# Later weight fetches tied to units, one pair of heads whole in batches 0 and 1, another estimate for transposes

## The chip, the cores and the metric

The kernel runs on one core of a Trainium2 chip. The core has engines that run side by side, each through its own instructions in their order: TensorE (PE in the profile; PEld is its weight load) multiplies matrices, VectorE (DVE), ScalarE (ACT) and GpSimd (POOL) work on elements, and SyncE (SP) here issues the DMAs. The metric is the time of one execution on the device in microseconds (us).

## The reference

Attention in which a query sees only the keys of its own hash bucket, and behind it two dense layers with a squared ReLU:

```python
q_bits = (np.einsum('bhsd,dk->bhsk', q, proj) > 0).astype(np.int64)   # k likewise
q_bucket = np.sum(q_bits * powers, axis=-1)
mask = q_bucket[:, :, :, None] == k_bucket[:, :, None, :]
scores = scale * np.matmul(q, k.transpose(0, 1, 3, 2))
scores = np.where(mask, scores, -1000000000.0)
attn = np.exp(scores - np.max(scores, axis=-1, keepdims=True))
attn = attn / (np.sum(attn, axis=-1, keepdims=True) + 1e-09)
...
x = np.ascontiguousarray(attn_out.transpose(0, 2, 1, 3)).reshape(B * S, H * D)
h = np.maximum(x @ w_in, 0.0)
return (h * h @ w_out).astype(np.float32)
```

There are 4 batches, 8 heads, 768 tokens and 64 elements in a head; `x` is 3072 x 512, `w_in` 512 x 2048 and `w_out` 2048 x 512, drawn in float64 and brought to the chip as they are.

## The kernel before

The Python program records operations and doesn't issue them. `Program.add` (line 148) notes each operation with the buffers that it reads and writes, the engines that could do it ("ways"), and a rank. `order` (222) then plans: `forward` (295) places operations in time on five queues by the estimated costs of `cost` (174) and one estimate for all DMA, `backward` (251) gives priorities from the end of that plan, and of five rounds the one with the shortest planned span is kept. `emit` (376) issues each engine's operations in the planned order. What the planner believes of a duration thus changes no instruction, only their order on each engine, and for operations with several ways the engine. The emitted program keeps the true dependences of data; each engine takes its instructions in the order given.

**Units and visits.** The attention of one head is done in two halves of 384 queries, each in three units of 128. A `unit` (651) makes scores `pS` on PE, their negated maximum `nmx` on DVE, `e` = exp with its sum on ACT, the reciprocal `rv`, two fp16 parts `hl` (ACT, then DVE), and a transposing DMA from `hl` to `aT`. There are 192 units. A visit is a pair of heads and one half, so six units. Behind them `av` (679) multiplies `aT` with the values `VV` into `pA` and leaves two parts in `xx`. `prep` (564) makes a pair's operands `A`, `L`, `Q` and `M`, of which two buffers each exist. In batch 0 it is "plain": one prep takes one buffer of each (its first head `A` and `L`, its second `Q` and `M`), so the last two preps are alive. A later prep takes both buffers of all four, and only the last is alive. When the next visit's pair is no longer alive, `ready` (792) prepares it again.

The order of visits (785 to 788): `WHOLE` says of how many pairs of a batch both halves come one after the other. The other pairs come first with half 0, and then, backwards, with half 1. Batches that aren't named have all four pairs whole. Before, batch 0 has two whole pairs: its order is pair 0 both halves, 1 both halves, 2 and 3 with half 0, 3 and 2 with half 1.

**The MoE.** When all four pairs of a batch's half are done, `moe` (696) runs a stage, eight in all. A stage has 16 blocks of `w_in`: `pm` on PE, then `g32` and the two parts `g` on ACT and DVE, and the second layer into `po`. A step is a group of three matmuls; a block has four steps into `pm` and three into `po`, so a stage has 112 steps, and the kernel 896. `pace` (770) ties step m to a unit u by the points of `PACE`: the planner places the step only after that unit's first matmul. Beyond the last point steps are free. Only the first stage finds weights that aren't aligned yet: it sums four blocks at a time into `acc`, and `align` (546) then scales `wo` in place.

**Weights.** Each layer has four groups of four tiles. `fetch` (489) loads a 512 KB tile of raw 64-bit numbers (`raw`, two buffers), takes sixteen bits of each (`top`, on DVE or POOL), and makes `f` on DVE; `split` (515) squares the four `f` on ACT (`sq`), adds them on PE (`pt`) for a scale, and writes two fp16 parts into `win` or `wo`. Group 0 and 1 of `w_in` and group 0 of `w_out` are recorded behind the first three visits (`WIN_AT`, `WOUT_AT`), the others inside the first stage (757 to 763), all with ranks of their own.

**Around it.** While the planned order leaves PE idle ahead of the first `pm`, `emit` fills in `idle` matmuls. In odd units below `ALTERNATE`, `pS` uses the PSUM space of `po`.

Of the kernel before, what the change touches and what calls it, by code (L numbers as in the profile page):

```python
# [40 lines left out]
ROUNDS, BEHIND = 4, 40000  # L41

PREP, STACKS, VALUES = -9, 0, 2
WIN_RANK, WOUT_RANK = (18, 2.0), (30, 2.5)
RANK_PE, RANK_MOE = 1e6, -1.0

PLAIN, ALTERNATE = 4, 36

WHOLE = {0: 2}


WIN_AT, WOUT_AT = (0, 2), 1
FIRST = len(WIN_AT)

PACE = ((25, 0), (64, 120), (193, 640))

IDLE_FROM, IDLE_SHARE = 1000, 0.6

# [54 lines left out]
class Program:  # L113
# [59 lines left out]
    @staticmethod  # L173
    def cost(key, name, args, kw):

        size = lambda x: int(np.prod(x.shape[1:]))
        column = {F32: 4 / 2.4, F32R: 0.445}
        if name == "matmuls":

            side = {32: 4, 64: 2}.get(size(args[0][0][1]), 1)  # L180
            t = sum(size(a[2]) * column.get(a[2].dtype, 1 / 2.4) + 7 for a, _ in args) / side
            return t, t
        kinds = [x.rec.kind if isinstance(x, View) else "" for x in args]
        ptr = any(isinstance(x, View) and x.shape[-1] == 1 for x in args[2:3])
        n = max(size(args[0]), size(args[1]) if isinstance(args[1], View) else 0)
        if key == "pe":
            t = max(107, size(args[2]) * column.get(args[2].dtype, 1 / 2.4) + 3)
            return t, t
        if name.startswith("dma"):
            b = int(np.prod(args[0].shape)) * mybir.dt.size(args[0].dtype)  # L190
            inside = name == "dma_start_transpose" or kinds[:2] == ["sb", "sb"]
            busy = 1040 if key == "pool" else (650 if inside else 475) + 50 * (key == "act")
            return busy, b / (175 if name == "dma_start_transpose" else 314)
        if key == "act":
            t = 93 * (isinstance(kw.get("scale"), View) + isinstance(kw.get("bias"), View)) + (51 if "psum" in kinds[:2] else 93) + n / 1.2 + 93 * ("accum_out" in kw)
        elif key == "pool":
            t = 147 + n * (2.1 if args[0].dtype == F32 or args[0].dtype == F32R else 1.88) if name == "tensor_tensor" else 161 + n / 1.2 + 83 * ptr
        else:
            fast = name in ("tensor_copy", "tensor_scalar") and "psum" not in kinds[:2]
            both = len(args) > 3 and isinstance(args[3], View) and args[3].shape[-1] == 1  # L200
            t = 67 + n / (1.92 if fast else 0.96) + 62 * (ptr and (fast or name == "scalar_tensor_tensor")) + 100 * both
        return t, t
# [212 lines left out]
def lsh_attention_moe(ctx: ExitStack, tc, kq, v, proj2, w_in, w_out, consts, out):  # L415
# [10 lines left out]
    def send(out, x):  # L426
        sp.dma_start(out, x)
# [58 lines left out]
        dve.memset(x.bitcast(F32), 0.0)  # L486
    turn = [0]

    def fetch(src):

        raw = sb([P, 512, 2], U32, "raw", BUFS["raw"])
        send(raw.rearrange("p n t -> p (n t)").bitcast(U16)[:, 0:2047], src.bitcast(U16)[:, 1:2048])
        first = tops[turn[0] % len(tops)]
        turn[0] += 1
        move(first[:, :, 1], raw.rearrange("p n t -> p (n t)").bitcast(BF16).rearrange("p (n t) -> p n t", t=4)[:, :, 2], 1.0, (dve, pool))
        f = sb([P, 512], F32, "f")
        dve.scalar_tensor_tensor(f.bitcast(U32), raw[:, :, 0], 13, first.rearrange("p n t -> p (n t)").bitcast(U32), ALU.logical_shift_right, ALU.bitwise_or)
        return f
# [13 lines left out]
        dve.tensor_scalar(back, norm, 2.0**50, 1.0, ALU.mult, ALU.mult)  # L512
        return to, back

    def split(srcs, parts, name):

        fs = [fetch(src) for src in srcs]
        pt = ps([P, 512], F32, "pt", tag="misc")
        for n, f in enumerate(fs):
            sq = sb([P, 512], BF16, "sq", 2)  # L520
            square(sq, f)
            pe.matmul(pt, ones, sq, start=n == 0, stop=n == len(fs) - 1)
        norm = sb([P, 1], F32, "norm")
        dve.tensor_reduce(norm, pt, AX.X, ALU.max)
        to, back = scales(norm, name, 4)
        for f, (hi, lo) in zip(fs, parts):
            move(hi, f, to)
            left(lo, f, to, hi)
        return to, back
# [2 lines left out]

    def split_win(j):
        w = slice(j * 512, (j + 1) * 512)
        win_back.append(split([w_in[:, cc, w] for cc in range(NCC)], [(win[:, 0, cc, w], win[:, 1, cc, w]) for cc in range(NCC)], "win")[1])

    def split_wout(j):

        back = split([w_out[:, n] for n in range(4 * j, 4 * j + 4)], [(wo[:, 0, n], wo[:, 1, n]) for n in range(4 * j, 4 * j + 4)], "wo")[1]
        z = zs[:, j : j + 1]  # L540
        dve.tensor_scalar(z, back, win_back[j], win_back[j], ALU.mult, ALU.mult)

# [153 lines left out]
    def moe(n, b, half):  # L696
# [5 lines left out]
        for f in range(NF + 1):  # L702
            if f < NF:
                pr.rank = RANK_PE
                pm = ps([P, 512], F32, "pm", 1)
                pr.busy_from = min(pr.busy_from, len(pr.ops))
                for cc in reversed(range(NCC)):
                    pr.mark = pace()
                    wh = win[:, 0, cc, f * P : (f + 1) * P]
                    wl = win[:, 1, cc, f * P : (f + 1) * P]  # L710
                    pe.matmul(pm[:, 0:HS], wh, X[cc][:, 0], start=cc == NCC - 1, stop=False)
                    pe.matmul(pm[:, 0:HS], wh, X[cc][:, 1], start=False, stop=False)
                    pe.matmul(pm[:, 0:HS], wl, X[cc][:, 0], start=False, stop=cc == 0)
                pr.rank, pr.mark = RANK_MOE, None

                g32 = sb([P, HS], F32, "g32", 2)
                pr.add((act, "activation", (g32, pm[:, 0:HS], AF.Relu), {"scale": 2.0**-23}),
                       (dve, "tensor_scalar", (g32, pm[:, 0:HS], 2.0**-23, 0.0, ALU.mult, ALU.max), {}))
                square(g32, g32)
                g = gs[f] = sb([P, 2, HS], F16, "g")  # L720
                move(g[:, 0], g32)
                left(g[:, 1], g32, 1.0, g[:, 0])

            if f > 0:
                m = f - 1
                g = gs.pop(m)
                pr.mark = None
                first, last = (m % 4 == 0, m % 4 == 3) if n == 0 else (m == 0, m == NF - 1)
                if first:
                    po = ps([P, 3, DM], F32, "po")  # L730
                for t in range(3):
                    gh = g[:, 0, t * P : (t + 1) * P]
                    gl = g[:, 1, t * P : (t + 1) * P]
                    pr.rank, pr.mark = RANK_PE, pace()
                    pe.matmul(po[:, t], gh, wo[:, 0, m], start=first, stop=False)
                    pe.matmul(po[:, t], gh, wo[:, 1, m], start=False, stop=False)
                    pe.matmul(po[:, t], gl, wo[:, 0, m], start=False, stop=last)
                    pr.mark = None
                pr.rank = RANK_MOE
                if n == 0 and last:  # L740
                    back = unscaled(b, m // 4)
                if n == 0 and m == 3:
                    acc = sb([P, 3, DM], F32, "acc")
                for t in range(3):
                    r0 = b * S + half * HS + t * P
                    if n == 0 and last:
                        if m == 3:
                            move(acc[:, t], po[:, t], back)
                        else:
                            dve.scalar_tensor_tensor(acc[:, t], po[:, t], back, acc[:, t], ALU.mult, ALU.add)  # L750
                        if m == NF - 1:
                            send(out[r0 : r0 + P], acc[:, t])
                    elif last:
                        o = sb([P, DM], F32, "o", tag="f")
                        move(o, po[:, t], back)
                        send(out[r0 : r0 + P], o)
            if n == 0 and f in (1, 5, 9):
                j = f // 4 + FIRST
                if j < 4:
                    pr.rank = win_rank(4 * j)  # L760
                    split_win(j)
                pr.rank = conv_rank(f + 3)
                split_wout(f // 4 + 1)
        if n == 0:
            pr.rank = RANK_MOE
# [4 lines left out]
    def pace():  # L770
# [3 lines left out]
            if m < m1:  # L774
                return int(u0 + (u1 - u0) * (m - m0) / (m1 - m0))
        return None

    def conv_rank(f):
        return WOUT_RANK[0] + WOUT_RANK[1] * f

    def win_rank(c):
        return WIN_RANK[0] + WIN_RANK[1] * c


    visits = []
# [11 lines left out]

    ready(*visits[0][:2], -10.0, PLAIN > 0)

    early = {n: (split_win, j, win_rank(4 * j)) for j, n in enumerate(WIN_AT)}  # L800
    early[WOUT_AT] = split_wout, 0, conv_rank(0)
    done, u, stages = {}, 0, 0
    for n, (b, hp, half) in enumerate(visits):
        sts, aTs = kept[b, hp], []
# [56 lines left out]
```

## Time and profile before

| what | us |
|---|---|
| median of 3 runs | 925.9 |
| lowest and highest of them | 923.61 and 926.62 |
| the profiled execution | 925.36 |
| its span, from the first to the last instruction | 923.6 |
| first `pm` of the MoE | 169.5 |
| DVE busy | 643.8 |
| ACT busy | 663.6 |

A row of a timeline has start, duration, engine, line, operation, what it writes and reads, and a count. A row of groups has a count, the busy time, the mean in ns, and the idle time in front of it with what ended that. A row of windows has the stretch, its length, each engine's busy time with instructions in brackets, PE's granted clock, the DMA engines' busy share and GB/s; asked for one tile, it counts that tile's instructions alone. As one helper records everything, most instructions have line 402, pairs of matmuls line 399 and idle matmuls line 395, so tiles tell more than lines.

### The profile page before, as it was taken

Reading aid. Unit: us, or ns where it says so; the run is one execution under the profiler, and the core shown is the slowest. Engines: PE = TensorE matmul, PEld = TensorE weight load, DVE = VectorE, ACT = ScalarE, POOL = GpSimd, SP = SyncE. Lnnn points to the kernel's source line nnn. Section 1 sums busy time; section 2 is a strip of 40 time slices with the busy share of each in tenths; the row PEclk is TensorE's granted clock in tenths of the full one; section 3 lists DMA queues with packets and bytes.
Section 4 is the critical chain, followed back from the end, with each engine's and each line's share of the span. In section 5 each row is a group of like instructions: output and inputs, shape, how many; then the busy total and the mean of one; then the engine's idle time right before and its main releaser. Section 6 shows DMA issues by size and latency. Waiting matters only on the chain.

```text
span 923.6 us, 15264 instructions
## 1 busy us (share of the span) xinstructions
PE 885.6 (96%) x5592; PEld 501.3 (54%) x5592; DVE 643.8 (70%) x1206; ACT 663.6 (72%) x1166; POOL 54.8 (6%) x104
## 2 busy tenths in 40 slices
PE   7988988999997999999999999999999999999997
PEld 6555555445554555555555556555555555554553
DVE  5999999988979687889686768797867651211111
ACT  4877987878879677888777768787778673533433
POOL 0111301200103000000000000000000000000000
PEclk9999999999999999999999999999999999999999
DMA  7998999997999797999697959897878640200000
GB/s 236 248 222 210 226 237 213 250 211 193 236 203 242 133 192 148 185 234 244 145 198 159 190 121 198 174 213 154 170 149 177 121 102 10 77 1 0 35 1 35
DMA packets 329323, 149.99 MB, mean 162 GB/s; under 512 B 305568, under 2 KB 305696, under 8 KB 329248
## 3 DMA queue, kind: packets, MB, share of 16 engines
q1 hardware_dynamic: 329248, 149.02, 73.6%
q8 instruction: 44, 0.72, 0.3%
q14 instruction: 31, 0.25, 0.1%
HBM read 43.59 MB, written 6.29 MB: 54 GB/s over the span
## 4 chain that ended last, share of the span: by engine, by line
PE 63%; ACT 5%; DMA 2%; DVE 2%; issue 1%; POOL 0%; SPq 0%; ACTq 0%; DVEq 0%
PE po L402 23%; PE pm L402 21%; PE pS L402 9%; PE pA L399 8%; ACT wo L402 1%; DMA aT<-hl 1%; ACT e L402 1%; PE pd L399 1%; DMA RV<-vp 1%; ACT hl L402 1%; DVE hl L402 1%; ACT g L402 1%; PE pc L402 1%; DVE nmx L402 1%; DMA M<-Q 1%
## 5 line engine op out<-in xcount | busy, mean ns | idle before, releaser
L402 PE MATMUL po<-wo,g 128*128 128x512 f16 x1152 | 332.7, 381 | 2.7 <-ACT wo L402 0.9
L402 PE MATMUL pm<-xx,win 128*128 128x384 f16 x1536 | 322.4, 327 | 1.3 <-DVE g L402 1.0
L402 DVE TENSOR_REDUCE nmx<-pS 128x1 f32<-128x768 f32 x192 | 183.1, 954 | 57.7 <-PE pS L402 56.6
L402 ACT ACTIVATE e<-pS,nmx 128x768 f32<-128x768 f32 x192 | 171.6, 894 | 67.8 <-DVE nmx L402 48.8
L402 DVE SCALAR_TENSOR_TENSOR hl<-e,rv,hl 128x768 f16<-128x768 f32 x192 | 194.1, 1012 | 26.1 <-ACT hl L402 25.5
L402 PEld LDWEIGHTS <-win 128*128 128x128 f16 x1536 | 145.1, 98 | 115.4 <-issue 17.8
L402 ACT ACTIVATE hl<-e,rv 128x768 f16<-128x768 f32 x188 | 173.5, 928 | 25.1 <-ACT e L402 14.0
L402 PEld LDWEIGHTS <-g 128*128 128x128 f16 x1152 | 107.9, 98 | 131.3 <-issue 26.4
L402 DVE SCALAR_TENSOR_TENSOR g<-g,g 128x384 f16<-128x384 f32 x122 | 67.5, 554 | 127.7 <-ACT g L402 127.1
L402 ACT ACTIVATE g<-pm 128x384 f32<-128x384 f32 x125 | 60.7, 486 | 108.3 <-PE pm L402 107.4
L402 ACT ACTIVATE g<-g 128x384 f32<-128x384 f32 (+1 forms) x248 | 128.8, 520 | 10.8 <-PE po L402 5.6
L399 PE MATMUL pA<-aT,VV 128*64 128x384 f16 x1152 | 117.8, 331 | 0.0
L402 PE MATMUL pS<-A,Q 128*128 128x384 f32 x288 | 95.2, 411 | 5.0 <-ACT e L402 4.8
L399 PEld LDWEIGHTS <-VV 128*64 128x64 f16 x1152 | 59.5, 109 | 55.8 <-issue 35.8
L402 PE MATMUL pS<-L,M 128*128 128x384 f32 x288 | 77.8, 350 | 0.2
L402 PEld LDWEIGHTS pS<-A,Q 128*128 128x128 f32 x288 | 49.3, 190 | 29.8 <-ACT e L402 15.9
L402 POOL TENSOR_SCALAR rv<-sm 128x1 f32<-128x1 f32 x74 | 28.8, 389 | 610.6 <-ACT e L402 604.0
L395 PEld LDWEIGHTS <-ones 128*128 128x128 bf16 x756 | 49.9, 103 | 20.1 <-issue 11.8
L395 PE MATMUL idle<-ones 128*128 128x128 bf16 x756 | 54.7, 228 | 2.7 <-DVE ones L402 2.7
L402 PEld LDWEIGHTS pS<-L,M 128*128 128x128 f32 x288 | 51.9, 189 | 3.9 <-issue 2.4
L402 PE MATMUL pS<-Q,M 128*128 128x384 f32 x96 | 37.3, 510 | 9.5 <-ACT e L402 9.1
L402 PE MATMUL pS<-A,L 128*128 128x384 f32 x96 | 36.6, 508 | 5.7 <-ACT e L402 5.4
(92 smaller groups left out, 579.9 us busy)
## 6 DMA issues: line engine op xcount, KB each, us to landing
RV<-vp SPq DMA_DIRECT2D x32, 384.0 KB
R<-kq SPq DMA_DIRECT2D x24, 384.0 KB
raw<-w_in SPq DMA_DIRECT2D x16, 511.8 KB
raw<-w_out SPq DMA_DIRECT2D x16, 511.8 KB
out<-o SPq DMA_DIRECT2D x21, 256.0 KB
Q<-L SPq DMA_DIRECT2D x24, 192.0 KB
Q<-A SPq DMA_DIRECT2D x24, 192.0 KB
L<-M SPq DMA_DIRECT2D x24, 192.0 KB
```

The lines of the kernel that those rows point to most:

```text
L395: issue(q, q.engine.matmul(self.idle[0].real(), self.idle[1].real(), self.idle[1].real(), start=True, stop=True).ins)
L399: ins = q.engine.matmul(*map(real, args), **kw).ins
L402: ins = getattr(q.engine, o.name)(*map(real, o.args), **{k: real(x) for k, x in o.kw.items()}).ins
```

## The change

- `WHOLE` is `{0: 1, 1: 1}`: in batches 0 and 1 one pair is whole, and the other three have half 0 first and half 1 backwards.
- Every fetch of a weight tile gets a mark: the planner places the load behind the first matmul of the unit in `WIN_FROM` or `WOUT_FROM` for its group. The ranks of the groups are listed one by one. As with `pace`, the mark is a dependence of the plan alone.
- ACT may take `top`.
- `PACE` runs in one line from unit 20 to 700 steps at unit 193.
- `ALTERNATE` ends at unit 30.
- The planner's bandwidth for a transposing DMA is 292 bytes per ns where it was 175.

```diff
-WIN_RANK, WOUT_RANK = (18, 2.0), (30, 2.5)
+WIN_RANK, WOUT_RANK = (18, 20, 28, 34), (20, 25, 31, 37)
+
+WIN_FROM, WOUT_FROM = (0, 18, 25, 31), (8, 22, 28, 34)
...
-PLAIN, ALTERNATE = 4, 36
-
-WHOLE = {0: 2}
+PLAIN, ALTERNATE = 4, 30
+
+WHOLE = {0: 1, 1: 1}
...
-PACE = ((25, 0), (64, 120), (193, 640))
+PACE = ((20, 0), (193, 700))
...
-            return busy, b / (175 if name == "dma_start_transpose" else 314)
+            return busy, b / (292 if name == "dma_start_transpose" else 314)
...
-    def fetch(src):
+    def fetch(src, since):
 
         raw = sb([P, 512, 2], U32, "raw", BUFS["raw"])
+        pr.mark = since
         send(raw.rearrange("p n t -> p (n t)").bitcast(U16)[:, 0:2047], src.bitcast(U16)[:, 1:2048])
+        pr.mark = None
...
-        move(first[:, :, 1], raw.rearrange("p n t -> p (n t)").bitcast(BF16).rearrange("p (n t) -> p n t", t=4)[:, :, 2], 1.0, (dve, pool))
+        move(first[:, :, 1], raw.rearrange("p n t -> p (n t)").bitcast(BF16).rearrange("p (n t) -> p n t", t=4)[:, :, 2], 1.0, (act, dve, pool))
...
-    def split(srcs, parts, name):
-
-        fs = [fetch(src) for src in srcs]
+    def split(srcs, parts, name, since):
+
+        fs = [fetch(src, since) for src in srcs]
...
                 if j < 4:
-                    pr.rank = win_rank(4 * j)
+                    pr.rank = WIN_RANK[j]
                     split_win(j)
-                pr.rank = conv_rank(f + 3)
+                pr.rank = WOUT_RANK[f // 4 + 1]
                 split_wout(f // 4 + 1)
...
-    early = {n: (split_win, j, win_rank(4 * j)) for j, n in enumerate(WIN_AT)}
-    early[WOUT_AT] = split_wout, 0, conv_rank(0)
+    early = {n: (split_win, j, WIN_RANK[j]) for j, n in enumerate(WIN_AT)}
+    early[WOUT_AT] = split_wout, 0, WOUT_RANK[0]
```

`split_win` and `split_wout` hand `WIN_FROM[j]` and `WOUT_FROM[j]` on to `split`; `conv_rank` and `win_rank` are gone.

More of the change, by code (lines that the diff above doesn't have):

```diff
@@ L534, in split_win @@
         w = slice(j * 512, (j + 1) * 512)
-        win_back.append(split([w_in[:, cc, w] for cc in range(NCC)], [(win[:, 0, cc, w], win[:, 1, cc, w]) for cc in range(NCC)], "win")[1])
+        win_back.append(split([w_in[:, cc, w] for cc in range(NCC)], [(win[:, 0, cc, w], win[:, 1, cc, w]) for cc in range(NCC)], "win", WIN_FROM[j])[1])
     def split_wout(j):
-        back = split([w_out[:, n] for n in range(4 * j, 4 * j + 4)], [(wo[:, 0, n], wo[:, 1, n]) for n in range(4 * j, 4 * j + 4)], "wo")[1]
+        back = split([w_out[:, n] for n in range(4 * j, 4 * j + 4)], [(wo[:, 0, n], wo[:, 1, n]) for n in range(4 * j, 4 * j + 4)], "wo", WOUT_FROM[j])[1]
         z = zs[:, j : j + 1]
@@ L776, in pace @@
         return None
[L778 to L782, printed above, removed]
     visits = []
```

## The prediction

> **What bounds the kernel now.** I read the page first: the span and the engines' row.
>
> ```profile
> span 923.6 us, 15264 instructions
> PE 885.6 (96%) x5592; PEld 501.3 (54%) x5592; DVE 643.8 (70%) x1206; ACT 663.6 (72%) x1166; POOL 54.8 (6%) x104
> ```
>
> TensorE (PE) is the engine to read, but 96% hides two stages. The windows show them (columns: busy PE, PEld, DVE, ACT, POOL; clock; DMA).
>
> ```profile
> 25.00:50.00 25.00, 22.75 (x177) 14.20 (x177) 24.80 (x51) 20.27 (x36) 4.40 (x9) 1.00 1.05 222
> 138.00:169.50 31.50, 26.57 (x251) 17.59 (x246) 30.10 (x61) 22.78 (x40) 5.07 (x8) 1.00 1.06 220
> 169.50:300.00 130.50, 122.93 (x730) 67.12 (x728) 118.21 (x228) 113.00 (x190) 18.27 (x31) 0.99 0.97 222
> 300.00:740.00 440.00, 438.50 (x2674) 247.59 (x2672) 336.10 (x607) 342.15 (x613) 11.64 (x26) 1.00 0.84 174
> L395 PE MATMUL idle<-ones 128*128 128x128 bf16 x756 | 54.7, 228 | 2.7 <-DVE ones L402 2.7
> DVE nmx L402 <- PE pS L402: 2.2, 6, 0.5
> ```
>
> Up to 169.5 us VectorE (DVE) is the bound: 24.80 of 25 us busy, and still 30.10 of 31.5 at the end; the longest of its waits between 25 and 169.5 us, the last row, comes to 2.2 us. TensorE's busy time there includes 756 idle matmuls, placed only ahead of the first `pm`. At 169.5 us the MoE begins, and from there TensorE is the bound.
>
> That it is full after 300 us I check by its work, not by its busy share. The prices first, from starts of neighbouring rows on PE, then the counts of matmuls.
>
> ```profile
> 59.13 1.56 PE L402 MATMUL pS<-Q,M 128*128 128x384 f32 x4
> 60.52 0.38 PE L402 MATMUL pt<-sq,ones 128*128 128x512 bf16 x1
> 60.74 2.45 PE L395 MATMUL idle<-ones 128*128 128x128 bf16 x41
> ...
> 70.97 3.12 PE L399 MATMUL pA<-aT,VV 128*64 128x384 f16 x36
> 74.02 0.39 PE L402 MATMUL pt<-sq,ones 128*128 128x512 bf16 x1
> ...
> 191.72 0.85 PE L399 MATMUL pd<-R,pj 128*32 128x384 f32 x8
> 192.50 1.15 PE L402 MATMUL pm<-xx,win 128*128 128x384 f16 x6
> ...
> 292.00 0.62 PE L402 MATMUL pS<-A,Q 128*128 128x384 f32 x2
> ...
> 292.81 1.96 PE L402 MATMUL pm<-xx,win 128*128 128x384 f16 x11
> ```
>
> A plain unit (batch 0) costs 60.52-59.13 = 1.39 us, an `av` 74.02-70.97 = 3.05, a `pt` of 512 columns 60.74-60.52 = 0.22, the `pd` of a prep 0.78 and its four `pc`, bf16 as `pt` but 384 wide, 0.22 x 384/512 = 0.16 each, so a prep 1.4, and a later unit 292.81-292.00 = 0.81.
>
> ```profile
> 300.00:740.00 440.00, 161.41 (x804) 1.00 0.84 174
> 760.00:910.00 150.00, 100.92 (x428) 1.00 0.07 19
> 300.00:740.00 440.00, 171.49 (x624) 1.00 0.84 174
> 760.00:910.00 150.00, 102.82 (x317) 1.00 0.07 19
> 300.00:740.00 440.00, 120.23 (x456) 1.00 0.84 174
> 300.00:740.00 440.00, 70.33 (x680) 1.00 0.84 174
> 760.00:910.00 150.00, 9.67 (x72) 1.00 0.07 19
> 300.00:740.00 440.00, 7.67 (x72) 1.00 0.84 174
> ```
>
> These are, in pairs, `pm` and `po`, then `pS`, `pA` (two) and `pd`. A step is three matmuls. From 760 to 910 us: (428+317)/3 = 248 steps in 150 us less two `av` and a last bit of `pS` (7), so 0.58 us a step. From 300 to 740 us: 476 steps x 0.58 = 276, 114 units x 0.81 = 92, 18.9 `av` x 3.05 = 58, 9 preps x 1.4 = 13. The sum is 439 of 440 us: PE is full. So only two things shorten this kernel: useful PE work done ahead of 169.5 us, and the 130.5-122.93 = 7.6 us in which PE stands still between 169.5 and 300.
>
> **The change, part by part.** *WHOLE.* In batch 0 the first half's fourth pair now comes with the fifth visit, not the sixth: 30 units instead of 36 ahead of MoE stage 0. When is that?
>
> ```profile
> 0.00:126.60 126.60, 30.34 (x30) 0.99 0.97 228
> 134.11 1.00 PE L399 MATMUL pA<-aT,VV 128*64 128x384 f16 x10
> 161.71 1.98 PE L399 MATMUL pA<-aT,VV 128*64 128x384 f16 x22
> 169.50 1.30 PE L402 MATMUL pm<-xx,win 128*128 128x384 f16 x7
> ```
>
> The first counts DVE's `hl`: the 30th ends at 126.6 us. From the 30th to its `av` took 134.1-126.6 = 7.5 us, and from the sixth `av` to the first `pm` 169.5-161.7 = 7.8. So 126.6+15.3 = 142 us, if DVE has done the same by then.
>
> *Top of the weights on ACT, marks, ranks.* DVE's own share before that point changes a little.
>
> ```profile
> L402 DVE TENSOR_SCALAR top<-raw 128x512 f16<-128x512 bf16 x16 | 7.3, 454 | 0.4 <-DMA raw<-w_in 0.3
> L402 DVE SCALAR_TENSOR_TENSOR f<-raw,top 128x512 uint32<-128x512 uint32 x28 | 19.4, 697 | 0.0
> L402 DVE SCALAR_TENSOR_TENSOR win<-f,towin,win 128x512 f16<-128x512 f32 x16 | 12.0, 770 | 0.8 <-POOL win L402 0.8
> L402 ACT ACTIVATE sq<-f 128x512 bf16<-128x512 f32 x28 | 17.1, 623 | 4.3 <-DVE f L402 3.4 <-DVE towin L402 0.5
> ```
>
> (All up to 169.5 us.) ACT's `top` isn't in the trace. Its nearest row is `sq` of the same width, 0.62 us; the bounds are 0.48 (`top` on DVE, 0.45, and a little) and 1.03 (on POOL, from the groups). ACT idles 31.5-22.78 = 9 of the 31.5 us before 169.5, which hides some 14 of them; DVE loses up to 9 of its 16, so 4 us. A weight group costs DVE 4 x (0.70+0.77) and its scale, near 6.5 us; seven of eight groups are read by 169.5 us, and the new marks (units 0 to 34) lie before the units at which most are read now, so they hold little back. The marks are dependences of the planner alone, no wait on the chip: a fetch moves to another place in SP's queue, ahead of or behind some transposes, which it can hold up (the longest transpose below is 5.6 us); that lies in the next bounds and in the gaps. One group more or less by unit 30, is plus or minus 6.5. I take 142-4 = **138 us** (131 to 146) for the MoE's start.
>
> What does 31.5 us earlier bring? PE does useful work there already:
>
> ```profile
> 138.00:169.50 31.50, 10.90 (x28) 1.00 1.06 220
> 138.00:169.50 31.50, 4.46 (x52) 1.00 1.06 220
> 138.00:169.50 31.50, 2.48 (x7) 1.00 1.06 220
> ```
>
> `pS` 28/4 x 1.39 = 9.7, `pA` 52/36 x 3.05 = 4.4, seven `pt` x 0.22 = 1.5: 15.6 us. Free are 31.5-15.6 = **15.9 us**, half a microsecond per microsecond of earlier start: 12 to 20 for the bounds.
>
> *Extra preps.* Each plain prep takes one of two buffers of A, L, Q, M; a later one takes two. So batch 0 prepares pair 1 twice (5 preps for 4), and batch 1 pairs 2 and 1 twice (6 for 4): three more, **+4.2 us** of PE. Their loads and moves on SP, DVE (four `M` at 0.67, and twice 1.03 for `L` where not plain) and ACT lie beside a full PE.
>
> *Stage 0 and the gaps.* Units, weights and MoE now crowd together in 138 to 300 us. ACT was busy 113 of 130.5 us there, and the 16 us of `wo` alignment stay. Before, PE lost 7.6 us; I take 11, bounds 4 and 18 (both DVE and ACT near 90%): **+3.4 us**.
>
> *PACE, ALTERNATE.* More MoE released per unit moves work from a full tail into a full stretch: 0, unless a stage isn't ready (a rival). ALTERNATE ends with the start of `po`'s use, as before: 0. Idle matmuls end with the earlier `pm`; without them the clock was 0.99 from 169.5 to 300 us, so 0.
>
> *The transposes' estimate* moves no instruction's cost, only where the planner puts `pA`.
>
> ```profile
> L402 SPq DMA_TRANSPOSE aT<-hl x192: 1273/1495/5576, 26.2 to 793.7; - x192
> L399 PE MATMUL pA<-aT,VV 128*64 128x384 f16 x1152 | 117.8, 331 | 0.0
> ```
>
> A transpose holds SP 1.50 us at the median. The old estimate is 393216/175 = 2.25 us, the new 1.35: better, but now below the measured. PE never waited for `aT` (0.0). Six transposes a visit times 0.15 are 0.9 us that a late `pA` could cost; the sixth `pA` stood 12.7 us behind its transposes, so I count 0 and keep 3 us for the whole kernel in the range. The Trainium skill ("DMA: Bandwidth & Descriptors", Latency and other measured facts) gives 261 GB/s for a transpose with a non-contiguous middle dimension; as an estimate that is 1.51 us, and speaks against the 292 of this change. The trace's median agrees with the page; by it the sum would be at most these 3 us more.
>
> Sum: -15.9 +4.2 +3.4 = -8.3. The profiled execution took 925.4 us (span 923.6), the median is 925.9: **917 us**.
>
> **The rivals.** *Given back.* With the new PACE, step 448, the first of stage 4 (batch 2, first half), is released at unit 20+448 x 173/700 = 131, but its `xx` needs unit 137 and some 3 units for transposes and `av`. If MoE runs some 4 units behind its marks, 5 to 6 units run without it. There a unit takes DVE's time, 336.1/114 less its share of `g` (0.3) = 2.6 us, for 1.4 us of PE: 7 us lost, and 1 more at stage 2. 917+8 = 925 us, no change. For it speaks the count; against it that the planner's backward pass may run units ahead.
>
> *Slower: batch 1's preps on six-unit visits.* A prep's first stack can take its buffers only when three units of the visit before are left, 3 x 440/114 = 11.6 us.
>
> ```profile
> 236.10 0.53 SPq L402 DMA_DIRECT2D Q<-A  x1
> 245.55 5.14 DMA M<-Q
> ```
>
> The chain from the first copy to the landing of `M<-Q` took 245.55+5.14-236.10 = 14.6 us, 3.0 more than that, and stands on the critical chain. Now five hand-overs of batch 1 come after six units, at a busy DMA (0.97). If PE finds no MoE in its order there, they cost 5 x 3.0 = 15 us: 932 us. It decides from 2 us a hand-over.
>
> *The start doesn't move.* The planner keeps the best of five rounds by its own clock; if weights come first, the MoE waits as now and the preps alone are left: 925.4+4.2 = 929.6 us.
>
> **How the numbers follow.** Forecast (907 to 923) 0.54, given back 0.19, slower by the preps 0.19, no earlier start 0.08. A measurement tells 0.3% (2.8 us) from no change. The forecast is faster but for 0.01 of it, which is the same; given back is same; the two others are slower but for 0.03. Faster 0.53, same 0.23, slower 0.24. The range leaves out a tenth at each end: the start at 131 us with small gaps gives 917-4-4 = 909, with a little more from the gaps 907; above it takes in the no-start case and half of the slower one: 907 to 932.
>
> **What would show it.** First `pm` between 131 and 146 us; 30, not 36, `hl` needed; 152 `pd` instead of 128; no idle matmuls behind that; PE without waits for `M<-Q` between 220 and 380 us, and no thin PE windows where batch 2's first half ends (some 500 to 560 us); `pA` with no idle time. A first `pm` after 155 us, or over 15 us of PE idle time behind it, would make the prediction wrong.

## The result, and the profile after

The changed kernel takes 954.15 us (median; 952.94 to 957.63) where the kernel before takes 925.62 in the same comparison: a ratio of 1.0317, with an interval of 1.0284 to 1.0351. It is 3% slower, and the forecast was 917, 907 to 932. The first page of the kernel after:

```profile
span 951.4 us, 15021 instructions
PE 888.4 (93%) x5420; PEld 488.2 (51%) x5421; DVE 648.5 (68%) x1196; ACT 689.5 (72%) x1213; POOL 37.8 (4%) x94
```

PE's busy time is nearly what it was (885.6 before), the span 27.8 us longer. Where the time went is seen in two more views of the kernel after. First the tile `pm` on PE: matmuls, least, median and longest ns, and the first and last start.

```profile
L404 PE MATMUL pm<-xx,win x1536: 322/326/543, 141.6 to 942.0; 128*128 128x384 f16 x192
```

The MoE begins at 141.6 us, 28 us earlier than before. Then the windows of the kernel after (length, PE, PEld, DVE, ACT, POOL, clock, DMA):

```profile
138.00:169.50 31.50, 29.94 (x161) 15.36 (x156) 30.65 (x62) 31.04 (x58) 3.46 (x7) 1.00 1.05 269
169.50:300.00 130.50, 121.74 (x694) 64.04 (x691) 110.30 (x211) 109.67 (x185) 11.77 (x19) 0.97 0.90 189
300.00:740.00 440.00, 418.00 (x2535) 232.75 (x2536) 326.82 (x585) 328.32 (x588) 13.77 (x34) 1.00 0.90 180
```

From 300 to 740 us PE is busy for 418.0 us where it was 438.5. Busy time flatters it; the work tells more. The same stretch of the kernel after, asked for `pm`, `po`, `pS`, `pA` and `pd` in turn:

```profile
300.00:740.00 440.00, 151.19 (x744) 1.00 0.90 180
300.00:740.00 440.00, 155.67 (x559) 1.00 0.90 180
300.00:740.00 440.00, 112.56 (x436) 1.00 0.90 180
300.00:740.00 440.00, 68.90 (x674) 1.00 0.90 180
300.00:740.00 440.00, 9.61 (x80) 1.00 0.90 180
```

By the prediction's prices: (744+559)/3 = 434 steps x 0.58 = 252, 436/4 = 109 units x 0.81 = 88, 674/36 = 18.7 `av` x 3.05 = 57, 10 preps x 1.4 = 14. That is 411 us of work in 440, where the kernel before did 439. So the work fell by 6.2%, PE's busy time by 4.7. The weight loads (PEld, 247.59 us before, 232.75 after) fell by 6.0. The Trainium skill ("Perfetto Trace Analysis", Identifying the Most-Contended Engine) holds the busy share of weight loads for a better measure than that of matmuls; this trace agrees. The clock is 1.00 in both, so it isn't that. From 138 to 300 us the same counting (without the preps) has the changed kernel do 6 us more, 139.8 us of work against 133.9; ahead of 138 us it had done 3 less, 67.2 against 70.1. Behind 740 us it does 204 us of work in 211.4, where the kernel before does 179 in 183.6, so it loses 3 us more there. **Nearly the whole loss lies between 300 and 740 us.** What PE and PEld wait for there, in the kernel after (us in all, times, longest):

```profile
PE pS L404 <- DMA M<-Q: 10.3, 12, 1.7
PE pS L404 <- ACT e L404: 7.7, 11, 3.1
PE pA L401 <- DMA aT<-hl: 1.7, 1, 1.7
...
PEld pS L404 <- ACT e L404: 17.1, 29, 3.5
PEld pS L404 <- DMA M<-Q: 7.0, 5, 2.1
```

and all that the same view says of PE, and of `e` and this copy for PEld, in the kernel before:

```profile
PE pS L402 <- ACT e L402: 1.4, 3, 0.8
...
PEld pS L402 <- ACT e L402: 7.5, 22, 1.1
...
PEld pS L402 <- DMA M<-Q: 0.2, 1, 0.2
```

The new wait is for `M<-Q`, the last copy in a prep's chain through SP's queue. The waits for `e` grow too, but they don't go with the loss: from 169.5 to 740 us PE waits 5.6 us for `e` in the kernel before, 7.7 in the changed one, and 6.7 in a kernel below that loses nothing (292 with slack). The groups of the kernel after show the second new thing, idle time ahead of `pA`, which had 0.0 before:

```profile
L401 PE MATMUL pA<-aT,VV 128*64 128x384 f16 x1152 | 123.8, 334 | 6.9 <-DMA aT<-hl 6.9
L404 PE MATMUL pS<-L,M 128*128 128x384 f32 x288 | 79.1, 355 | 12.7 <-DMA M<-Q 12.6
```

Three of the parts can bring such waits: the estimate for transposes (the plan puts DMA's results too early), batch 1's order (more preps, later), and the new pace (other work in between). The theory was the first, the rival the second.

### The profile page after: what moved, and what is told of

It is laid out like the page before. It is cut to its first block, busy times and chain, and to the rows that moved or that the text cites. A ratio compares the mean times of both kernels' runs of the same rounds, so it can differ in the third digit from the quotient of the medians.

```text
span 951.4 us, 15021 instructions
## 1 busy us (share of the span) xinstructions
PE 888.4 (93%) x5420; PEld 488.2 (51%) x5421; DVE 648.5 (68%) x1196; ACT 689.5 (72%) x1213; POOL 37.8 (4%) x94
## 5 line engine op out<-in xcount | busy, mean ns | idle before, releaser
L404 PE MATMUL po<-wo,g 128*128 128x512 f16 x1152 | 340.4, 382 | 3.5 <-ACT acc L404 1.6
L404 PE MATMUL pm<-xx,win 128*128 128x384 f16 x1536 | 328.5, 328 | 1.4 <-ACT g L404 1.2
L404 ACT ACTIVATE hl<-e,rv 128x768 f16<-128x768 f32 x190 | 175.9, 930 | 38.1 <-DMA aT<-hl 20.7
L401 PE MATMUL pA<-aT,VV 128*64 128x384 f16 x1152 | 123.8, 334 | 6.9 <-DMA aT<-hl 6.9
L404 PE MATMUL pS<-L,M 128*128 128x384 f32 x288 | 79.1, 355 | 12.7 <-DMA M<-Q 12.6
L404 PEld LDWEIGHTS pS<-A,Q 128*128 128x128 f32 x288 | 49.2, 190 | 31.5 <-ACT e L404 18.3
L404 POOL TENSOR_SCALAR rv<-sm 128x1 f32<-128x1 f32 x82 | 29.2, 356 | 685.3 <-ACT e L404 682.2
L397 PEld LDWEIGHTS <-ones 128*128 128x128 bf16 x549 | 35.2, 100 | 21.6 <-issue 14.6
L404 DVE TENSOR_SCALAR M<-pc,cst 128x384 fp32r<-128x384 f32 (+1 forms) x66 | 44.2, 670 | 1.2 <-PE pc L404 1.2
```

What stands on the lines that cost most here:

```text
L397: issue(q, q.engine.matmul(self.idle[0].real(), self.idle[1].real(), self.idle[1].real(), start=True, stop=True).ins)
L401: ins = q.engine.matmul(*map(real, args), **kw).ins
L404: ins = getattr(q.engine, o.name)(*map(real, o.args), **{k: real(x) for k, x in o.kw.items()}).ins
```

## The experiments: the estimate

The number of the estimate alone, once taken out of the changed kernel and once put into the kernel before:

```diff
 # the changed kernel
-            return busy, b / (292 if name == "dma_start_transpose" else 314)
+            return busy, b / (175 if name == "dma_start_transpose" else 314)
 # the kernel before
-            return busy, b / (175 if name == "dma_start_transpose" else 314)
+            return busy, b / (292 if name == "dma_start_transpose" else 314)
```

> The changed kernel with the planner's old transpose estimate, 175 bytes per ns, alone put back. Theory T (the shorter estimate places operations on PE too soon behind their DMAs, so that PE, which takes its instructions in order, waits for M<-Q and aT through the whole attention): the waits for M<-Q and aT nearly go, PE busy from 300 to 740 us comes back from 418.0 towards 438 us, and the time falls by 15 to 30 us, to 925 to 940. Rival W (batch 1's and 0's repeated preps): stays above 948. Rival P (the new pace runs into stages that aren't ready): stays above 948.

> The kernel before with the new transpose estimate, 292 bytes per ns, alone. Theory T: 15 to 30 us slower than before (940 to 956), with PE waiting for M<-Q and aT after 300 us as in the changed kernel. Rivals W and P: within 5 us of before, or a little faster by the shorter way from hl to the first pm.

Measured: 935.17 us against 923.92 for the kernel before (1.0124, 1.0109 to 1.0139) and 943.36 (1.0209, 1.0166 to 1.0252). Set against the kernel before of the same comparison, the changed kernel loses 28.5 us, and 11.3 with the old number; the kernel before loses 19.4 with the new one. (Losses are given in this way from here on.) **The number is worth 17 to 19 us, whether it is taken out of the one kernel or put into the other.** It is a belief of the planner and changes no instruction's cost. The kernel before with it shows the waits, between 169.5 and 740 us:

```profile
PE pS L402 <- ACT e L402: 7.8, 11, 2.0
PE pS L402 <- DMA M<-Q: 6.7, 9, 1.4
PE pd L399 <- DMA R<-kq: 4.6, 2, 3.5
...
PE pS L402 <- DMA A<-A: 1.4, 1, 1.4
```

In the changed kernel PE waits 12.6 us for `M<-Q` in this stretch, and with the old number

```profile
PE pS L404 <- DMA M<-Q: 1.7, 3, 1.3
```

Is it that this order is bad, or only that it has no margin? If margin, then the new estimate with time added in the plan between a DMA's landing and PE's use of it should do as well as the old one. `LAGS` holds the planner's delays between engines; 200 ns is its default.

```diff
 # the kernel before, with 292; the same line then in the changed kernel
-        ("act", "dve"): 100, ("act", "pool"): 180, ("pool", "dve"): 70, ("pool", "act"): 50, ("pool", "sp"): 140}
+        ("act", "dve"): 100, ("act", "pool"): 180, ("pool", "dve"): 70, ("pool", "act"): 50, ("pool", "sp"): 140, ("sp", "pe"): 2200}
```

> The kernel before with the new transpose estimate, 292, and in the plan 2 us more between any SP DMA's landing and the PE instruction that uses it. It gave 943 without that slack. Theory T (the loss of the estimate is PE waiting in order for DMAs that land later than planned): the margin of pA behind its last transpose grows from some 1 us to some 3, the PE waits for M<-Q, R<-kq and aT fall, and the time is 922 to 932. Rival T2 (the shorter estimate harms through what it makes the planner do with the other engines, not through the margin ahead of PE): 938 or more.

> The changed kernel with 2 us more in the plan between any SP DMA's landing and its PE instruction; everything else as changed. Theory T (margin): it comes down like the changed kernel with the old estimate, to 928 to 938, and PE's idle time from 300 to 740 us (22 us) falls to some 8; what then is left over 925 is batch 1's repeated preps. If the estimate hurts here in another way: 945 or more.

In the kernel before the time is all back: 924.73 us against 924.53 (1.0008, 0.9991 to 1.0025). PE's waits for `M<-Q` between 169.5 and 740 us shrink to

```profile
PE pS L402 <- DMA M<-Q: 0.3, 1, 0.3
```

and PE's busy time between 300 and 740 us comes back in part. The windows of this kernel, behind the windows of the one with 292 alone:

```profile
300.00:740.00 440.00, 426.53 (x2606) 243.36 (x2604) 340.08 (x608) 338.94 (x612) 17.11 (x37) 1.00 0.93 181
```

```profile
300.00:740.00 440.00, 434.30 (x2622) 241.29 (x2619) 332.24 (x599) 331.91 (x596) 17.48 (x33) 1.00 0.89 172
```

So the old estimate, 2.25 us for what takes 1.50, acted as a margin: without it PE waits for DMA, and time added openly in the plan takes these waits away. It doesn't bring back the old course, though. By the prediction's prices, counted from the start, the kernel with slack has done 224.8 us of work at 300 us and 654.3 at 740, with 292 alone it is 208.7 and 633.1, and in the kernel before 213.7 and 652.3. So 16 of the 21 us that the slack wins by 740 us are won ahead of 300 us, and between 300 and 740 us this kernel still does 9 us less than the kernel before.

From the packets of the transposing DMA the time between a visit's last transposed packet and its first `pA` can be worked out: its median is 5.1 us in the kernel before, 0.5 with 292, and 3.1 with the added 2 us. A smaller margin there need not cost anything: it is 3.0 in the kernel with batch 0's order alone, the fastest of those below. In the changed kernel the slack brings back 9.5 of 17: 942.98 us against 923.98 (1.0211, 1.0173 to 1.0248).

Is it the transposes that come late? Then slack for them alone would do:

```diff
 # the kernel before, with 292
-                done = dma + 910 - t
+                done = dma + 910 + 2000 * (o.name == "dma_start_transpose") - t
```

> The kernel before with the estimate 292 and 2 us of slack in the plan behind the landing of transposes alone, not of SP's other copies. If pA behind its transposes is the margin that matters: 922 to 929, as with slack for all. If the copies of the preps (M<-Q, R<-kq), queued on SP behind the transposes, are what comes late: 936 to 945.

It wins 7 of the 19: 934.7 us against 922.68 (1.0124, 1.0099 to 1.015). The margin in front of `pA` is 5.2 us, as before the change. PE's waits for `aT` were only 1.8 us with 292 alone, and they are gone; the 7 us are won ahead of 300 us, where this kernel has done 216.2 us of work against 208.7. PE still waits for the other copies (169.5 to 740 us):

```profile
PE pS L402 <- DMA M<-Q: 9.4, 9, 1.8
PE pS L402 <- DMA A<-A: 2.3, 1, 2.3
PE pd L399 <- DMA R<-kq: 1.6, 2, 0.9
```

These come to 13.3 us, against 12.7 for the same three with 292 alone; with slack for all of SP's DMA they are 0.3. **The larger part of the estimate's harm goes through the copies that stand in SP's queue among the transposes.** The planner lets all DMA pass one after the other; when six transposes of a visit become 0.90 us shorter each in the plan, whatever stands behind them is planned up to 5.4 us earlier.

A control: any other number reshuffles the order too, and differences could be luck.

```diff
 # the kernel before
-            return busy, b / (175 if name == "dma_start_transpose" else 314)
+            return busy, b / (180 if name == "dma_start_transpose" else 314)
```

> The kernel before with an estimate of 180 bytes per ns instead of 175, as a control: a change too small to alter any margin by more than 0.06 us a transpose reshuffles the order a little. By theory T 922 to 928. If the planner's orders scatter widely by themselves, so that single variants tell little, it can lie 5 us or more away from 925.

923.26 us against 923.98 (0.9996, 0.9983 to 1.001). The order did change: of the 192 units PE begins only 24% after the same number of MoE steps as in the kernel before, hardly more than the 22% with 292. So this reshuffle by itself moves nothing; it is one sample.

## The experiments: order, weights and pace

The orders of visits. First the old order in the changed kernel, then each batch's new order alone in the kernel before:

```diff
 # the changed kernel, the old order
-PLAIN, ALTERNATE = 4, 30
+PLAIN, ALTERNATE = 4, 36
-WHOLE = {0: 1, 1: 1}
+WHOLE = {0: 2}
 # the kernel before, batch 0's new order
-PLAIN, ALTERNATE = 4, 36
+PLAIN, ALTERNATE = 4, 30
-WHOLE = {0: 2}
+WHOLE = {0: 1}
 # the kernel before, batch 1's new order
-WHOLE = {0: 2}
+WHOLE = {0: 2, 1: 1}
```

> The changed kernel with the old order of visits (two whole pairs in batch 0, all in batch 1; ALTERNATE 36 with it): no prep is repeated. Theory T: the first pm goes back to some 155 to 165 us, the waits after 300 us stay, and the time is 945 to 960. Rival W: three preps and their hand-overs are gone, and the time falls to 925 to 935. Rival P: 945 to 955.

> The kernel before with one whole pair in batch 0 (ALTERNATE 30 with it), nothing else. The theory of the prediction: the first pm comes some 15 to 25 us earlier, one prep more costs 1.4 us, and the time falls by 3 to 10 us to 914 to 921. Rival: the work brought forward is given back before 300 us or by waits behind it, 922 to 930.

> The kernel before with one whole pair in batch 1 (batch 0 as before): two preps more, hand-overs after six units. By PE's work alone 2.8 us more, 925 to 928. Rival W (each hand-over makes PE wait some 3 us): 932 to 940, with PE waits for M<-Q between 200 and 400 us.

The old order in the changed kernel: 938.05 us against 923.92 (1.0154, 1.0138 to 1.0171), a loss of 14.1 where the change as it is loses 28.5. But this run holds a loss of another kind. Its first `pm` is back at 169.9 us; its windows for `pm` (`po` has one matmul in the second):

```profile
0.00:383.00 383.00, 72.30 (x384) 0.99 0.88 202
383.00:402.00 19.00, 0.00 (x0) 0.64 0.67 166
```

The MoE stands still at step 224, by PE's rows for 20.0 us from 382.8 us. The same stop is taken apart below, and it comes from the new pace with batch 1's old order. What the orders cost without it this run doesn't tell. **Batch 0's order alone: 920.45 us against 924.53 (0.996, 0.9947 to 0.9974), faster than both kernels and the best of the study.** Its first `pm` and its windows:

```profile
L402 PE MATMUL pm<-xx,win x1536: 323/326/338, 151.5 to 910.2; 128*128 128x384 f16 x192
```

```profile
300.00:740.00 440.00, 436.56 (x2669) 246.74 (x2667) 340.71 (x615) 345.59 (x619) 15.92 (x34) 1.00 0.85 179
```

The MoE begins 18 us earlier and the later stretch stays full. Batch 1's order alone: 934.06 us (1.0113, 1.0091 to 1.0136), 9.5 us lost, of which two more preps are 2.8. In its waits, 169.5 to 740 us, the copy of the longer hand-over stands first, though here the estimate is the old one:

```profile
PE pS L402 <- DMA M<-Q: 6.8, 5, 2.8
```

The weights' part alone (marks, ranks, `top` on ACT), which is the changed kernel with the other four lines set back:

```diff
 # the changed kernel
-PLAIN, ALTERNATE = 4, 30
+PLAIN, ALTERNATE = 4, 36
-WHOLE = {0: 1, 1: 1}
+WHOLE = {0: 2}
-PACE = ((20, 0), (193, 700))
+PACE = ((25, 0), (64, 120), (193, 640))
-            return busy, b / (292 if name == "dma_start_transpose" else 314)
+            return busy, b / (175 if name == "dma_start_transpose" else 314)
```

> The kernel before with the marks of the fetches, their new ranks and top on ACT as well; order of visits, pace and estimate as before. If these parts matter little: 920 to 928. If top on ACT makes ACT the bound ahead of the MoE: the first pm comes later than 169.5 us and the time is over 930.

924.52 us against 924.53 (1.000, 0.9985 to 1.0015): nothing. The first `pm` comes at 162.8 us, 7 earlier, which it doesn't turn into time.

The pace, the old one in the changed kernel and the new one in the kernel before:

```diff
 # the changed kernel
-PACE = ((20, 0), (193, 700))
+PACE = ((25, 0), (64, 120), (193, 640))
 # the kernel before
-PACE = ((25, 0), (64, 120), (193, 640))
+PACE = ((20, 0), (193, 700))
```

> The changed kernel with the old PACE alone. Theory T: 945 to 956, the waits for DMA after 300 us stay. Rival P: the loss after 300 us goes, 920 to 935. Rival W: 945 to 956.

> The kernel before with the new PACE alone. Rival P of the prediction: stage 4 isn't ready when its steps are released, so PE thins out and the time is 928 to 935. Without that: 922 to 927. If marking more steps early helps: under 922.

958.18 us against 923.92 (1.0375, 1.0356 to 1.0395) and 922.1 against 923.98 (0.9976, 0.9961 to 0.9991): with the old pace the changed kernel loses 34.3 us instead of 28.5, so the new one is worth 6 there, and 2 in the kernel before.

That leaves batch 0's order at -4, the pace at -2, the weights at 0 and batch 1's order at +9.5: a sum of +3.5 where the changed kernel with the old estimate has +11. And it promises something faster: batch 0's order with the new pace. Three kernels try it, without batch 1's order, and a fourth takes batch 0's order under the old pace, with the new estimate and slack:

```diff
 # the kernel before
-PLAIN, ALTERNATE = 4, 36
+PLAIN, ALTERNATE = 4, 30
-WHOLE = {0: 2}
+WHOLE = {0: 1}
-PACE = ((25, 0), (64, 120), (193, 640))
+PACE = ((20, 0), (193, 700))
 # the changed kernel; a second one with this line and 175 for 292
-WHOLE = {0: 1, 1: 1}
+WHOLE = {0: 1}
 # the kernel before; beside these lines the slack of 2200 as above
-PLAIN, ALTERNATE = 4, 36
+PLAIN, ALTERNATE = 4, 30
-WHOLE = {0: 2}
+WHOLE = {0: 1}
-            return busy, b / (175 if name == "dma_start_transpose" else 314)
+            return busy, b / (292 if name == "dma_start_transpose" else 314)
```

> The kernel before with one whole pair in batch 0 and the new PACE, nothing else. If the two gains add: 915 to 920, faster than both kernels. If they are the same time won twice: 920 to 923.

> The changed kernel with batch 1 in the old order again (all four pairs whole), batch 0 as changed, the estimate 292. If batch 1's order costs here what it cost in the kernel before (9.5 us): 942 to 947. If the two losses feed each other, since each repeated prep is five more SP copies whose landings come late: 930 to 940. If the estimate alone explains the loss: 950 or more.

> The same with the old estimate, 175: both suspects undone, while batch 0's order, the marks, top on ACT and the pace stay as changed. By the parts measured alone (-4 for batch 0, -2 for the pace, 0 for the weights) 917 to 922. If something else of the change costs time in company: 925 or more.

> The kernel before with one whole pair in batch 0, the estimate 292, and the 2 us of slack. If both gains of the start add up (first pm some 18 us earlier by the visits, 17 by the estimate with slack) and PE stays full: 910 to 918. If the work brought forward is given back as it was with the slack alone: 918 to 925.

All are slower than the kernel before. The first takes 936.91 us against 922.68 (1.0156, 1.0124 to 1.0189), the changed kernel without batch 1's order 940.36 (1.0193, 1.0155 to 1.0231), and the same with 175 even 948.24 (1.0274, 1.0245 to 1.0304). The windows of that last one, over all engines and then for `pm` (the third line is the same for `po`), say why:

```profile
350.00:400.00 50.00, 38.84 (x217) 22.30 (x215) 35.49 (x62) 33.86 (x58) 0.64 (x2) 0.86 0.95 182
...
0.00:380.00 380.00, 73.39 (x384) 1.00 0.98 209
380.00:395.00 15.00, 0.00 (x0) 0.55 0.77 148
```

and the same for its `po`, and for the `nmx` of DVE, of which there is one in a unit:

```profile
0.00:380.00 380.00, 72.52 (x288) 1.00 0.98 209
...
0.00:380.00 380.00, 85.50 (x90) 1.00 0.98 209
```

384 + 288 = 672 matmuls, so 224 steps and two whole stages, at 380 us; by PE's rows the MoE stands still for 23.3 us from 374.0 us. Stage 2 is batch 1's first half, and with four whole pairs that half is complete only behind unit 90 (48 + 42). The new pace releases step 224 at unit 20 + 224 x 173/700 = 75, the old one at unit 64 + (224 - 120) x 129/520 = 89. This is the prediction's rival "given back", one stage earlier. Batch 1's new order completes the half at unit 78, and the changed kernel with 175, which has it, makes no such stop: it has (408 + 290)/3 = 232 steps at 380 us. The new pace and batch 1's order belong together, and what each is worth alone doesn't add. The stop depends on how far the units have come: where PE has begun 88 units ahead of step 224, as here, it lasts 23.3 us; with 89 units (the changed kernel with the old order) 20.0, with 91 (batch 0's order with the new pace) 15.8, and with 92 (the changed kernel without batch 1's order, 292) 7.4. Under the old pace batch 0's order alone has 92 units there and stops for 7.7 us. The new pace alone in the kernel before has 96 units and no stop. So the kernel with 292 loses less here than the one with 175 because it meets the same gap with its units further on; why they are further on wasn't taken apart.

With batch 0's order, the old pace, and 292 with slack, the MoE begins earlier still (143.1 us), and the time is 930.71 us against 923.98 (1.0079, 1.0052 to 1.0106). The lead is given back by 300 us, where by the prices this kernel has done 208.9 us of work against 213.7 in the kernel before:

```profile
169.50:300.00 130.50, 117.89 (x669) 62.76 (x669) 110.93 (x215) 105.51 (x177) 9.16 (x21) 0.95 0.79 181
```

PE loses 12.6 us there where it lost 7.6 before. Beginning earlier didn't help here; that units couldn't follow is the likely reason, but no run tests it.

The last run gives the whole change the old estimate and the slack too:

```diff
 # the changed kernel
 # beside this line the slack of 2200 as above
-            return busy, b / (292 if name == "dma_start_transpose" else 314)
+            return busy, b / (175 if name == "dma_start_transpose" else 314)
```

> The changed kernel with the old estimate, 175, and 2 us of slack in the plan ahead of PE. If the 11 us that are left are late landings: 922 to 930. If they are the repeated preps and the planner's order on crowded DVE and ACT: 931 to 942.

944.33 us against 923.68 (1.0222, 1.0203 to 1.024): more margin is not always better. Its windows for `pm` (the second of them reads the same for `po`), and then for `po`:

```profile
0.00:583.00 583.00, 152.65 (x768) 0.99 0.97 205
583.00:600.00 17.00, 0.00 (x0) 0.60 0.95 180
```

```profile
0.00:583.00 583.00, 147.70 (x576) 0.99 0.97 205
```

768 + 576 is 448 steps: the MoE stands still in front of stage 4, by PE's rows for 20.5 us from 580.6 us, exactly where "given back" put it.

## Why the prediction was wrong

**The start** was right, and by its mechanism: the 30th `hl` of DVE ends at 122.4 us (126.6 - 4 = 122.6 forecast), and the first `pm` comes at 141.6 us for 138 (131 to 146). Useful PE work between 138 and 169.5 us rose from 15.9 to 29.2 us, by 13.3 for the 15.9 forecast. **The gaps** look right by busy time: 31.5 - 29.94 and 130.5 - 121.74 are 10.3 us between 138 and 300, for 11. By work they are 15.2 (162 us less 29.2 and 117.6), inside the bounds of 4 and 18; the kernel before loses 8.3 by the same measure, so they cost 6.9 and not 3.4. With the 3 us less that were done ahead of 138 us, the lead at 300 us is 3 us of work and not 15.9 - 3.4 = 12.5. So some 9 of the 37 us between forecast and result were missed in this part already.

**The transposes' estimate** is the step that failed: "so I count 0 and keep 3 us for the whole kernel". It is 17 to 19 us. Two things were wrong in it, and a third was weak. I compared the new number with the measured length (0.15 us short of 1.50), not with what the plan had held until then; it gave up 0.90 for each transpose. I asked only who waits for `aT`, not who stands behind it in the queue: most of the loss is `M<-Q` and its like. And I took the margin from one visit's sixth `pA`, 12.7 us, where the median over the visits from the last transposed packet to the first `pA` is 5.1 and falls to 0.5. "PE never waited for `aT` (0.0)" stays nearly true with 292 in the kernel before (1.8 us; 6.9 in the changed kernel), and yet 19 us are lost: it was the wrong question. That PE didn't wait for `M<-Q` either held under the old estimate only (6.7 us with 292).

**The extra preps** were sized by their PE work, 4.2 us, and what they add on SP, DVE and ACT was to "lie beside a full PE". Batch 1's order alone costs 9.5 us against 2.8 by that count. The rival "slower: batch 1's preps" had the mechanism, waits for `M<-Q`, and 15 us; 6.8 us of such waits are in the records. But the loss isn't confined to batch 1: by the same counting of work (without the preps) that kernel falls behind by 5.4 us from 300 to 400 us, 1.7 from 400 to 500 and 4.2 from 600 to 740. The wait explains much of it and not all.

**PACE** at 0 left out a gain of 6 in the changed kernel (2 in the kernel before). The rival "given back" is a real mechanism, seen at 224 and at 448 steps, but only in kernels whose MoE ran ahead of their units. The changed kernel itself makes no such stop, and PE is full from 560 to 600 us. **The weights** were 4 us of the earlier start, so some 2 us of time at half a microsecond each; alone they bring the first `pm` 7 us forward and no time.

The prediction named over 15 us of PE's idle time behind the first `pm` as what would make it wrong: there were some 10 up to 300 us and 22.0 between 300 and 740.

Put together, the 28.5 us are 17 for the estimate and 11 for the rest under the old estimate. Of the latter, single parts account for 3.5; the remainder comes from parts in company. What it is stays open (it isn't the stop at step 224 or 448, which the changed kernel doesn't make with either estimate), and so does why 2 us of slack bring back all 19 in the kernel before and only 9.5 in the changed one.

## What to carry to other kernels

In a schedule made ahead of time and issued in order, a cost that is estimated too high can be margin. Before it is made exact, give the same margin openly at the places that need it, and count what shares the queue with the operation, not only who reads its result. A resource that "nobody waits for" in a trace may owe this to the number that is about to be changed. Parts of a schedule change don't add: here an order and a pace that win 4 and 2 us alone cost 14 together, so measure pairs as well as single parts.

## What was not expected of the hardware

Where the MoE stood still and PE had only units and what belongs to them, its granted clock fell: 0.55 in the 15 us from 380 us, 0.64 in the 19 us from 383 us and 0.60 in the 17 us from 583 us, in the windows above, where the kernel before has 1.00 over both stretches of 50 us. What is left to do in a starved stretch is thus done at a lower clock as well. PE's rows where it happens in the first of these (the changed kernel with 175, without batch 1's order), with the idle time in front of a row in brackets:

```profile
377.34 0.61 PE L404 MATMUL pS<-A,Q 128*128 128x384 f32 x2 [2.26 <-ACT e L404]
377.79 0.51 PE L404 MATMUL pS<-L,M 128*128 128x384 f32 x2
380.38 1.01 PE L404 MATMUL pS<-A,Q 128*128 128x384 f32 x2 [2.07 <-ACT e L404]
381.19 0.84 PE L404 MATMUL pS<-L,M 128*128 128x384 f32 x2
```

The same two matmuls take 0.61 us and then 1.01. By the Trainium skill ("TensorE: Matmul & The Clock Gate", Part 1) the clock falls to half after an idle window of about 3.4 us. A mean of 0.55 fits a clock of one half, but no gap of PE was longer than 2.3 us here: gaps of 2.1 to 2.3 us in front of every unit were enough. How much work would have held the clock no run here shows.

A transpose also held SP for longer in several variants, by the tile `aT` on SP of the kernel after:

```profile
L404 SPq DMA_TRANSPOSE aT<-hl x192: 1272/1776/5187, 23.1 to 843.8; - x192
```

The median is 1.78 us where it was 1.50. It isn't the loss: in the kernel before with 292 and slack, which loses nothing, the median is 1.76.
